# Scatters through disjoint views, routing pieces and gathers moved up, and row numbers kept in order, in an attention and two-layer expert kernel

## The chip, the cores and the metric

One core of a Trainium2 chip runs the whole program. The metric is the device time of one execution in microseconds, from the first to the last instruction plus what lies around them. Engines are named as in the profile: PE is TensorE (matmul) with PEld for its weight loads, DVE is VectorE, ACT is ScalarE, POOL is GpSimd, and SP is SyncE, which here only issues DMAs.

## What is computed

A windowed attention with a few global columns feeds a dense layer with an ELU between two matrices, and its rows feed eight experts, each row going to at most one. In the second part, `x` is the dense layer's output (3072 rows of 512):

```python
do_compute = x @ w_skip > 0
xc = x[do_compute]
logits = xc @ w_gate                      # 8 experts
e_idx = np.argmax(logits, axis=1)
gate_w = softmax(logits)[row, e_idx]
for e in range(8):
    mask = e_idx == e
    h = np.maximum(xc[mask] @ w1[e], 0.0) # 512 -> 1024
    y[mask] = gate_w[mask, None] * (h @ w2[e])
out = x; out[do_compute] = xc + y
```

## The kernel before

The 3072 rows are worked in eight blocks `m` of 384 rows, three tiles of 128 rows each. The main loop (line 872) takes a block in 16 steps `f` of 128 hidden columns: `moe_h` (line 431) is 12 matmuls into `h`, ACT, DVE and POOL turn `h` into the two-part value `gs`, and `moe_y` (line 453) is 9 matmuls that add `gs` times the second matrix into three sums `y`; it runs two steps behind `moe_h` (`LAG`). Attention for the next block is spread over the same steps.

A block's sums are routed by `route` (line 490) in the steps of the next block. Its pieces are: `evac` (ACT copies `y` into a tile `yt` per 128 rows, and the row is written to `out`), `turn` (DVE splits `yt` into two halves, and SP issues a transposing DMA), `gate` (8 small matmuls for the logits of one tile, line 527; behind the third tile's stands `choose`, a run of small DVE instructions that ends in the one-hot tile `oh`, line 548, and the gate weight), `place` (9 small matmuls `rk` count ranks, and DVE makes of them the slot numbers `pos`, line 576), and `scatter` (line 581: POOL issues an indirect DMA that sends the 128 rows of one `yt` to their slots in `xg`, a DRAM tile with 256 rows for each expert). `ROUTE` (line 59) says which piece stands in which step, beginning with step 2. The last block is routed in `ex_tail`, where `ROUTE_LAST` (line 60) names the expert step of each piece.

Experts: `ex_gather` (line 630) loads 128 rows of an expert from `xg` into `yg` by a DMA on SP. `ex_tokens` (line 638) makes a two-part half precision tile `eyh` on DVE (lines 644 and 645; one buffer for all) and has it transposed into `eyT` by a DMA. `ex_first` (line 648) is 12 matmuls into `eh` from `eyT`, after which ACT (line 662) and DVE (line 664) make the two halves of `ehs`; `ex_second` (line 668) is 3 matmuls into `eo`, two steps behind. The third of those three needs the half that DVE makes. At an expert's last step `ex_second` also makes the result row tile on DVE (`eres`, line 684), turns the row numbers into integers (`ix`, line 686, which reads the gathered tile alone) and issues an indirect DMA to `out` on POOL.

`ex_tail` (line 691) first works the first 128 rows of experts 0 to 2 (steps `s_` 0 to 23, eight steps each), and then their second 128 rows (steps 24 to 47). The first 128 rows are known to be filled by the first seven blocks, so they are gathered before the last block is routed: at `f` 11 of the last block, with `ex_tokens` at `f` 13 (line 896). The second 128 rows of those experts are gathered behind the last block's scatters, at step 15, with `ex_tokens` at steps 22, 24 and 26 (lines 709 to 714). Experts 3 to 7 follow with both halves at once. All the while `prep` (line 865) loads and splits one half row of expert weights a step (`ew`, lines 623 and 624); its loads `er` stand in SP's queue too.

What order an engine works in is fixed when the program is compiled. A scheduler takes the instructions in the order of the code, but lets one that its model holds to be ready go ahead of one that is not, and puts in all waits that the tiles' reads and writes need. `pin` (line 72) holds an instruction behind the one written just before it on its engine. On the chip every engine then takes its own list strictly in that order. Two writes to the same DRAM tile are ordered: the later one's issue waits until the earlier one has landed.

Of the kernel before, what the change touches and what calls it, by code (L numbers as in the profile page):

```python
# [1 line left out]

# [10 lines left out]
U32 = DT.uint32  # L13
# [7 lines left out]
B, H, S, D = 4, 8, 768, 64  # L21
NT, DM, FF = 3072, 512, 2048
# [3 lines left out]
TB = 3  # L26
TN = TB * P
NM = NT // TN
# [28 lines left out]
EX_HALVES = (2, 2, 2, 2, 2, 2, 2, 2, 2, 2, 2, 3, 1, 2, 2, 2)  # L57

ROUTE = "ea,b,,cA,B,C,p,x,y,z".split(",")
ROUTE_LAST = {3: 'et', 7: 'A', 8: 'B', 9: 'C', 11: 'p', 12: 'sw'}  # L60


class Fast:
# [400 lines left out]
    def route_init(self):  # L464
        nc = self.nc
        self.wg = self.ct([P, ND, E + 1], F32, "wg")
        nc.sync.dma_start(self.wg[:, :, 0:E], self.a["moe2_w_gate"].rearrange("(c p) e -> p c e", p=P))
        nc.sync.dma_start(self.wg[:, :, E:E + 1], self.a["moe2_w_skip"].rearrange("(c p o) -> p c o", p=P, o=1))

        self.wgs = self.ct([P, ND, 2, E + 1], F16, "wgs")  # L470
        t = self.ct([P, ND, E + 1], F32, "wgt")
        nc.vector.tensor_scalar(t, self.wg, GS, None, ALU.mult)
        nc.vector.tensor_copy(self.wgs[:, :, 0, :], t)
        nc.vector.tensor_tensor(self.wgs[:, :, 1, :], t, self.wgs[:, :, 0, :], ALU.subtract)
        nc.vector.tensor_tensor(t, t, t, ALU.mult)
        self.wgm = self.ct([P, 2], F32, "wgm")
        nc.vector.tensor_reduce(out=self.wgm[:, 0:1], in_=t[:, :, 0:E], op=ALU.max, axis=AX.XY)
        nc.vector.tensor_reduce(out=self.wgm[:, 1:2], in_=t[:, :, E], op=ALU.max, axis=AX.X)
        self.esum = self.ct([P, TB], F32, "esum")
        nc.vector.memset(self.esum, 0.0)  # L480
        self.xg = self.dp.tile([E * CAP, ROW], F32, name="xg")
        z = self.zrow = self.mp.tile([P, ROW], F32, tag="yt", name="zrow", bufs=4)
        nc.gpsimd.memset(z[:, 0:DM + 1], 0.0)
        nc.gpsimd.memset(z[:, DM + 1:ROW], OOB)
# [5 lines left out]
    def route(self, m):  # L490

        nc, mp = self.nc, self.mp
# [87 lines left out]

        def scatter(t):
            nc.gpsimd.indirect_dma_start(
                out=self.xg[:, :], out_offset=bass.IndirectOffsetOnAxis(ap=pos.bitcast(U32)[:, t:t + 1], axis=0),
                in_=yts[t][:, :], in_offset=None, bounds_check=E * CAP - 1, oob_is_err=False)

        def write():
# [4 lines left out]
        if last:  # L591
# [2 lines left out]
                    lambda: [scatter(t) for t in range(TB)], write]  # L594
        ops = dict(e=evac, a=lambda: turn(0), b=lambda: turn(1), c=lambda: turn(2), A=lambda: gate(0), B=lambda: gate(1),
                   C=lambda: gate(2), p=place, x=lambda: scatter(0), y=lambda: scatter(1), z=lambda: scatter(2))
        return [lambda w=w: [ops[o]() for o in w] for w in ROUTE]


    def ex_load(self, e, k):  # L600
# [67 lines left out]
    def ex_second(self, e, f, tiles):  # L668
        nc = self.nc
        hs = self.ehs.pop((e, f, tiles[0]))  # L670
        for j, t in enumerate(tiles):
            if f == 0:
                tag, bufs = ("pv", 1) if (e % 2 and t if e >= NX else e + t == 0) else ("acc", 3)
                self.eo[(e, t)] = self.ps.tile([P, DM], F32, tag=tag, name=f"eo_{e}_{t}", bufs=bufs)
            for n, (s_, x) in enumerate(((0, 0), (0, 1), (1, 0))):
                nc.tensor.matmul(self.eo[(e, t)], hs[:, s_, j * P:(j + 1) * P],  # L676
                                 self.ew[(e, 4 + f // 2, f % 2)][:, x, :],
                                 start=(f == 0 and n == 0), stop=(f == F2 // P - 1 and n == 2))
        if f < F2 // P - 1:
            return  # L680
        for t in tiles:
            y = self.eyg.pop((e, t))
            r = self.mp.tile([P, DM], F32, tag="yT", name=f"eres_{e}_{t}", bufs=2)
            nc.vector.scalar_tensor_tensor(r, self.eo.pop((e, t)), y[:, DM:DM + 1], y[:, 0:DM], ALU.mult, ALU.add)  # L684
            ix = self.xp.tile([P, 1], I32, tag="ix", name=f"ix_{e}_{t}", bufs=2 * E)
            nc.vector.tensor_copy(ix, y[:, DM + 1:DM + 2])
            nc.gpsimd.indirect_dma_start(  # L687
                out=self.out[:, :], out_offset=bass.IndirectOffsetOnAxis(ap=ix.bitcast(U32)[:, 0:1], axis=0),
                in_=r[:, :], in_offset=None, bounds_check=NT - 1, oob_is_err=False)

    def ex_tail(self, prep, rest):
        both = tuple(range(CAP // P))
        steps = [(e, f, (t,)) for t in both for e in range(NX) for f in range(F2 // P)]
        n0 = len(steps)
        steps += [(e, f, both) for e in range(NX, E - 1) for f in range(F2 // P)]
        steps += [(E - 1, f, (t,)) for t in both for f in range(F2 // P)]
        flag = self.flag()
        nf = F2 // P
        pieces = dict(zip("etABCpsw", self.route(NM - 1)))
        for s_, (e, f, tiles) in enumerate(steps):  # L700
            for x in ROUTE_LAST.get(s_, ""):
                pieces[x]()
            if s_ == 0:
                self.htags = "s0", "s1", "h"
            if s_ == 3:
                self.htags = ("h",)
            if s_ == 13:
                self.htags = "h", "s0", "h", "s1"
            if s_ == 15:
                for x in range(NX):  # L710
                    self.ex_gather(x, 1)
            for x in range(NX):
                if s_ == 22 + 2 * x:
                    self.ex_tokens(x, 1)
            if s_ == n0 - 10:
                self.ex_gather(NX, 0)
            if s_ == n0 - 9:
                self.ex_gather(NX, 1)
            if s_ in (n0 - 5, n0 - 3):
                self.ex_tokens(NX, (s_ - n0 + 5) // 2)  # L720
            if len(tiles) == 2 and e + 1 < E:
                if f == 1:
                    for t in both:
                        self.ex_gather(e + 1, t)
                if f in (3, 5):
                    self.ex_tokens(e + 1, (f - 3) // 2)
            self.ex_first(e, f, tiles)
            if s_ and rest:

                self.moe_y(*rest.pop(0))  # L730
            for _ in tiles:
                prep()
            if s_ >= 40:
                next(flag, None)
            if s_ == len(steps) - 1:
                for _ in flag:
                    pass
                self.flag_sum()
            if s_ >= XLAG:
                self.ex_second(*steps[s_ - XLAG])  # L740
        for x in steps[-XLAG:]:
            self.ex_second(*x)
        self.flag_all()
# [80 lines left out]
    def program(self, ep, wp, ap):  # L824
# [26 lines left out]
        t = 0  # L851
# [20 lines left out]
        for s_, (m, f) in enumerate(steps):  # L872
            if m < NM - 1:
                for _ in range(A_STEPS[min(m, 1)].count(f)):
                    self.att_step(t)
                    t += 1
            if m == NM - 1 and f == 0:
                ap.release()
                self.xp = tc.alloc_tile_pool(name="xp", bufs=2)
                self.esums = self.xp.tile([P, 32 * E], F32, tag="esums", name="esums", bufs=1)  # L880
                self.emax = self.xp.tile([P, 2 * E], F32, tag="emax", name="emax", bufs=1)
                nc.gpsimd.memset(self.esums, 0.0)
                for k in range(2):
                    self.ex_load(0, k)
            while done[0] < 2 * f + 2 and m == 0:
                whalf()
            self.moe_h(m, f)
            if m == NM - 1:
                for _ in range(EX_HALVES[f]):
                    prep()  # L890
            if m == 0:
                for _ in range(2):
                    whalf()
            if pend:
                pend.pop(0)()
            if m == NM - 1 and f in (11, 13):
                assert not pend
                for e in range(NX):
                    (self.ex_gather if f == 11 else self.ex_tokens)(e, 0)
            if s_ >= LAG:  # L900
                self.moe_y(*steps[s_ - LAG])
            if m == 0 and f == 7:
                self.route_init()
            if NF // 2 <= s_ < NF // 2 + E * CAP // P:
                self.clear(s_ - NF // 2)
            c = s_ - 2 * NF
            if c == 0:
                self.w_load(0, "wc")
            if 0 < c <= 4 * NF and c % 2 == 0:
                self.w_check(*divmod(c // 2 - 1, 2))  # L910
            if f == LAG and m:
                pend = self.route(m - 1)
                pend.pop(0)()
# [274 lines left out]
```

## Time and profile before

| | us |
|---|---|
| three timed runs | 864.92, 870.45, 873.59 |
| their median | 870.45 |
| the profiled execution | 866.19 |
| its span, first to last instruction | 864.5 |

| engine | busy us | share of the span |
|---|---|---|
| PE | 817.8 | 95% |
| PEld | 479.4 | 55% |
| DVE | 571.4 | 66% |
| ACT | 530.0 | 61% |
| POOL | 174.5 | 20% |

The profile is of one execution. It lists for each instruction when it ran, how long its engine sat idle ahead of it and what ended that. [...] A wait for several things is put down to the one that came last.

### The profile page before, as it was taken

How to read it: one execution, taken by the hardware profiler on the slowest of the kernel's cores; microseconds unless marked ns; L12 is line 12 of the kernel's file. 1: busy time of each engine (PE TensorE's matmuls, PEld its weight loads, DVE VectorE, ACT ScalarE, POOL GpSimd, SP SyncE). 2: the span in 40 equal slices, each digit the busy share in tenths (PEclk: the TensorE clock that was granted, in tenths of full speed). 3: DMA queues.
4: the chain of work that ended last, by engine and by line, in shares of the span. 5: the costliest groups of instructions: out<-in, count | busy, mean ns of one | idle time of the engine just before them, and what ended most of it. 6: DMA issues, size and time to landing. Idle time of an engine off the chain costs nothing.

```text
span 864.5 us, 17637 instructions
## 1 busy us (share of the span) xinstructions
PE 817.8 (95%) x6233; PEld 479.4 (55%) x6233; DVE 571.4 (66%) x1951; ACT 530.0 (61%) x1310; POOL 174.5 (20%) x201
## 2 busy tenths in 40 slices
PE   6997989999999999999999999999998869999995
PEld 4773445555555555555555555555555637666663
DVE  6997997575467567556666765644666846878622
ACT  4775767777767677767776776645655425555311
POOL 1001112123222322321322232232231010101110
PEclk9997999999999999999999999999999988999998
DMA  7999973644686487688659656321646779779510
GB/s 293 256 298 253 245 217 91 132 111 102 201 205 162 137 214 142 175 191 189 152 139 229 154 124 146 77 51 43 189 154 159 228 225 211 247 242 275 157 44 26
DMA packets 185394, 148.80 MB, mean 172 GB/s; under 512 B 152208, under 2 KB 154256, under 8 KB 181200
## 3 DMA queue, kind: packets, MB, share of 16 engines
q1 hardware_dynamic: 182096, 141.59, 63.0%
q0 software_dynamic: 3200, 5.99, 1.9%
q8 instruction: 51, 0.84, 0.4%
q14 instruction: 47, 0.39, 0.2%
HBM read 94.82 MB, written 21.08 MB: 134 GB/s over the span
## 4 chain that ended last, share of the span: by engine, by line
PE 72%; DVE 11%; DMA 10%; issue 4%; POOL 1%; ACT 1%; SPq 0%; POOLq 0%; DVEq 0%; ACTq 0%
PE h L439 25%; PE y L460 24%; PE eh L660 7%; PE eo L676 6%; PE s L239 5%; PE pv L324 4%; DMA eyT<-eyh 3%; DMA xg<-yt,pos 2%; DMA yg<-xg 2%; DVE ew L624 2%; DVE wt L408 2%; DVE wt L409 1%; PE warm L354 1%; DMA xT<-xs 1%; DVE w L416 1%
## 5 line engine op out<-in xcount | busy, mean ns | idle before, releaser
L439 PE MATMUL h<-xT,w 128*128 128x384 f16 x1536 | 274.9, 329 | 4.1 <-DMA xT<-xs 4.1
L460 PE MATMUL y<-w,gs 128*128 128x512 f16 x1152 | 271.4, 381 | 0.0
L439 PEld LDWEIGHTS <-w 128*128 128x128 f16 x1536 | 146.8, 99 | 106.4 <-issue 9.7
L450 POOL TENSOR_TENSOR gs<-e,gs 128x384 f16<-128x384 f32 x128 | 126.1, 987 | 393.9 <-ACT gs L449 329.2
L460 PEld LDWEIGHTS <-gs 128*128 128x128 f16 x1152 | 110.8, 98 | 119.9 <-issue 2.7
L446 DVE SCALAR_TENSOR_TENSOR e<-e,h 128x384 f32<-128x384 f32 x128 | 70.4, 551 | 99.6 <-ACT e L444 94.1
L449 ACT ACTIVATE gs<-e 128x384 f16<-128x384 f32 x128 | 66.7, 522 | 86.1 <-DVE e L446 84.9
L253 ACT ACTIVATE p<-p,st 128x232 f32<-128x232 f32 (+1 forms) x192 | 89.2, 465 | 38.4 <-DVE st L248 37.7
L660 PE MATMUL eh<-eyT,ew 128*128 128x128 f16 (+1 forms) x1152 | 103.6, 243 | 7.6 <-DMA eyT<-eyh 5.6
L676 PE MATMUL eo<-ew,ehs 128*128 128x512 f16 x384 | 102.0, 388 | 8.1 <-DVE ehs L664 8.1
L660 PEld LDWEIGHTS <-ew 128*128 128x128 f16 x1152 | 88.7, 101 | 32.8 <-issue 6.7
L624 DVE SCALAR_TENSOR_TENSOR ew<-er,ew 128x512 f16<-128x512 f32 x128 | 90.5, 725 | 15.9 <-ACT ew L623 14.5
L443 ACT ACTIVATE e<-h 128x384 f32<-128x384 f32 x128 | 61.6, 481 | 58.5 <-PE h L439 54.5
L662 ACT ACTIVATE ehs<-eh 128x128 f16<-128x128 f32 (+1 forms) x96 | 29.9, 311 | 102.3 <-PE eh L660 99.8
L248 DVE CUSTOM_DVE_ANT_0 p<-s,tab 128x232 f32<-128x232 f32 (+1 forms) x192 | 67.1, 377 | 20.3 <-PE s L239 18.6
L623 ACT ACTIVATE ew<-er 128x512 f16<-128x512 f32 x128 | 75.4, 620 | 4.5 <-DMA er<-in_moe_w 4.2
L283 DVE TENSOR_TENSOR ph<-p,ph 128x464 f16<-128x464 f32 x68 | 43.1, 648 | 40.2 <-ACT ph L282 40.2
L444 ACT ACTIVATE e<-e 128x384 f32<-128x384 f32 x128 | 66.6, 520 | 2.5
L664 DVE SCALAR_TENSOR_TENSOR ehs<-eh,ehs 128x128 f16<-128x128 f32 (+1 forms) x96 | 31.9, 332 | 36.9 <-ACT ehs L662 36.7
L676 PEld LDWEIGHTS <-ehs 128*128 128x128 f16 x384 | 35.4, 99 | 36.7 <-DVE ehs L664 12.7
L687 POOL DMA_INDIRECT out<-eres,ix x16 | 16.9, 1053 | 161.9 <-DVE eres L684 117.7
L239 PE MATMUL s<-qh 64*128 64x232 f16 (+1 forms) x432 | 40.0, 254 | 3.1 <-DVE st L248 2.5
(171 smaller groups left out, 849.4 us busy)
## 6 DMA issues: line engine op xcount, KB each, us to landing
er<-in_moe_w SPq DMA_DIRECT2D x64, 512.0 KB
wr<-in_wf SPq DMA_DIRECT2D x16, 1024.0 KB
wc<-in_wf SPq DMA_DIRECT2D x16, 1024.0 KB
qk<-in_qk SPq DMA_DIRECT2D x20, 720.0 KB
out<-yt SPq DMA_DIRECT2D x24, 256.0 KB
rawv<-in_vp SPq DMA_DIRECT2D x21, 256.0 KB
xg<-zrow SPq DMA_DIRECT2D x16, 257.0 KB
yg<-xg SPq DMA_DIRECT2D x16, 257.0 KB
```

The costliest lines, as they stand in the source:

```text
L239: nc.tensor.matmul(sp[j], q[r, hp, KW:], k[r, hp, KW - w:KW], start=(x == 0), stop=(x == len(mm) - 1))
L248: nc.vector.tensor_tensor_reduce(pw[:, j, :], sp[j], self.tab[:, h, :] if i else self.tab0[:, h, :], -0.125, 3e38, ALU.add, ALU.min, st[:, ...
L253: nc.scalar.activation(pw[:, j, :], pw[:, j, :], AF.Exp, bias=st[:, 0, h:h + 1], scale=-1.0, accum_out=st[:, 1, h:h + 1])
L439: nc.tensor.matmul(hps, wi[:, s_, c, :], xT[:, x * ND + c, :], start=(n == 0), stop=(n == 3 * ND - 1))
L446: nc.vector.scalar_tensor_tensor(g, e, -HS, hps, ALU.mult, ALU.max, accum_out=self.gsum[:, m * NF + f:m * NF + f + 1])
L449: nc.scalar.activation(gs[:, 0], g, AF.Copy)
L450: nc.gpsimd.tensor_tensor(gs[:, 1], g, gs[:, 0], ALU.subtract)
L460: nc.tensor.matmul(self.ys[m][t], gs[:, s_, t * P:(t + 1) * P], wo[:, x, :], start=(f == 0 and n == 0), stop=(f == NF - 1 and n == 2))
L623: self.pin(nc.scalar.activation(w[:, 0], r, AF.Copy, scale=sc))
L624: nc.vector.scalar_tensor_tensor(w[:, 1], r, sc, w[:, 0], ALU.mult, ALU.subtract, accum_out=self.esums[:, c:c + 1])
L660: nc.tensor.matmul(hps, l, r, start=(i == 0), stop=(i == len(mm) - 1))
L676: nc.tensor.matmul(self.eo[(e, t)], hs[:, s_, j * P:(j + 1) * P], self.ew[(e, 4 + f // 2, f % 2)][:, x, :], start=(f == 0 and n == 0), sto ...
```

## The change

There are three edits.

1. The scatters write through `xgs`, three views of `xg` that are declared disjoint, one for each tile of a block. Scatters of different tiles are no longer ordered against each other; a gather still reads `xg` itself and waits for all three.
2. Pieces are moved. For the last but one block (`m` 6) the routing follows `ROUTE_NEXT`: the third `turn` stands one step earlier, the gates and `place` stay at `f` 5 to 8, and all three scatters stand at `f` 9 in place of 9, 10 and 11. The first gathers go from `f` 11 to 10 and their `ex_tokens` from 13 to 12. In `ROUTE_LAST` the gates go from steps 7, 8, 9 to 6, 7, 8, `place` from 11 to 9, the scatters from 12 to 10, and the write of the rows stays at 12. The second gathers go from step 15 to 13, and their `ex_tokens` from 22, 24 and 26 to 17, 20 and 23.
3. The row number conversion `ix` is pinned behind `eres`, the instruction written before it on DVE.

```diff
--- before.py
+++ after.py
@@ -2,6 +2,7 @@
 
 import concourse.bass as bass
 import concourse.tile as tile
+from concourse.bass_types import dram_disjoint_views
 from concourse import mybir
 from concourse._compat import with_exitstack
 from concourse.masks import make_identity
@@ -57,7 +58,8 @@
 EX_HALVES = (2, 2, 2, 2, 2, 2, 2, 2, 2, 2, 2, 3, 1, 2, 2, 2)
 
 ROUTE = "ea,b,,cA,B,C,p,x,y,z".split(",")
-ROUTE_LAST = {3: 'et', 7: 'A', 8: 'B', 9: 'C', 11: 'p', 12: 'sw'}
+ROUTE_NEXT = "ea,b,c,A,B,C,p,xyz".split(",")
+ROUTE_LAST = {3: 'et', 6: 'A', 7: 'B', 8: 'C', 9: 'p', 10: 's', 12: 'w'}
 
 
 class Fast:
@@ -479,6 +481,8 @@
         self.esum = self.ct([P, TB], F32, "esum")
         nc.vector.memset(self.esum, 0.0)
         self.xg = self.dp.tile([E * CAP, ROW], F32, name="xg")
+
+        self.xgs = dram_disjoint_views(self.xg[:, :], TB)
         z = self.zrow = self.mp.tile([P, ROW], F32, tag="yt", name="zrow", bufs=4)
         nc.gpsimd.memset(z[:, 0:DM + 1], 0.0)
         nc.gpsimd.memset(z[:, DM + 1:ROW], OOB)
@@ -580,7 +584,7 @@
 
         def scatter(t):
             nc.gpsimd.indirect_dma_start(
-                out=self.xg[:, :], out_offset=bass.IndirectOffsetOnAxis(ap=pos.bitcast(U32)[:, t:t + 1], axis=0),
+                out=self.xgs[t][:, :], out_offset=bass.IndirectOffsetOnAxis(ap=pos.bitcast(U32)[:, t:t + 1], axis=0),
                 in_=yts[t][:, :], in_offset=None, bounds_check=E * CAP - 1, oob_is_err=False)
 
         def write():
@@ -594,7 +598,7 @@
                     lambda: [scatter(t) for t in range(TB)], write]
         ops = dict(e=evac, a=lambda: turn(0), b=lambda: turn(1), c=lambda: turn(2), A=lambda: gate(0), B=lambda: gate(1),
                    C=lambda: gate(2), p=place, x=lambda: scatter(0), y=lambda: scatter(1), z=lambda: scatter(2))
-        return [lambda w=w: [ops[o]() for o in w] for w in ROUTE]
+        return [lambda w=w: [ops[o]() for o in w] for w in (ROUTE if m < NM - 2 else ROUTE_NEXT)]
 
 
     def ex_load(self, e, k):
@@ -683,7 +687,7 @@
             r = self.mp.tile([P, DM], F32, tag="yT", name=f"eres_{e}_{t}", bufs=2)
             nc.vector.scalar_tensor_tensor(r, self.eo.pop((e, t)), y[:, DM:DM + 1], y[:, 0:DM], ALU.mult, ALU.add)
             ix = self.xp.tile([P, 1], I32, tag="ix", name=f"ix_{e}_{t}", bufs=2 * E)
-            nc.vector.tensor_copy(ix, y[:, DM + 1:DM + 2])
+            self.pin(nc.vector.tensor_copy(ix, y[:, DM + 1:DM + 2]))
             nc.gpsimd.indirect_dma_start(
                 out=self.out[:, :], out_offset=bass.IndirectOffsetOnAxis(ap=ix.bitcast(U32)[:, 0:1], axis=0),
                 in_=r[:, :], in_offset=None, bounds_check=NT - 1, oob_is_err=False)
@@ -706,11 +710,11 @@
                 self.htags = ("h",)
             if s_ == 13:
                 self.htags = "h", "s0", "h", "s1"
-            if s_ == 15:
+            if s_ == 13:
                 for x in range(NX):
                     self.ex_gather(x, 1)
             for x in range(NX):
-                if s_ == 22 + 2 * x:
+                if s_ == 17 + 3 * x:
                     self.ex_tokens(x, 1)
             if s_ == n0 - 10:
                 self.ex_gather(NX, 0)
@@ -893,10 +897,10 @@
                     whalf()
             if pend:
                 pend.pop(0)()
-            if m == NM - 1 and f in (11, 13):
+            if m == NM - 1 and f in (10, 12):
                 assert not pend
                 for e in range(NX):
-                    (self.ex_gather if f == 11 else self.ex_tokens)(e, 0)
+                    (self.ex_gather if f == 10 else self.ex_tokens)(e, 0)
             if s_ >= LAG:
                 self.moe_y(*steps[s_ - LAG])
             if m == 0 and f == 7:
```

## Rows read from the trace of the kernel before

**Rows 1.** windows of 24 us: window, busy us (instructions) per engine, TensorE clock, DMA share, GB/s

```profile
192.00:216.00 24.00, 23.96 (x181) 12.91 (x180) 13.67 (x47) 18.05 (x45) 7.95 (x8) 1.00 0.47 107
...
648.00:672.00 24.00, 20.55 (x138) 12.00 (x136) 16.86 (x56) 13.81 (x30) 3.65 (x4) 0.93 0.63 165
...
696.00:720.00 24.00, 15.15 (x126) 9.76 (x125) 11.37 (x45) 7.32 (x19) 3.90 (x4) 0.72 0.84 202
```

**Rows 2.** the same windows, cut to 5 us

```profile
660.00:665.00 5.00, 4.89 (x33) 3.52 (x34) 3.71 (x10) 2.93 (x7) 0.91 (x1) 0.66 0.58 107
...
715.00:720.00 5.00, 5.00 (x47) 3.97 (x46) 3.06 (x14) 3.07 (x8) 0.00 (x0) 0.68 1.24 162
```

**Rows 3.** timeline of PE: start, us, what [idle before it, and who ended that]

```profile
422.54 2.11 PE L460 MATMUL y<-w,gs 128*128 128x512 f16 x9
...
660.11 2.68 PE L660 MATMUL eh<-eyT,ew 128*128 128x128 f16 x24 [2.56 <-DMA eyT<-eyh]
...
673.11 0.83 PE L660 MATMUL eh<-eyT,ew 128*128 128x128 f16 x12 [2.00 <-DVE ehs L664]
...
680.44 0.25 PE L530 MATMUL lg<-wgs,yTa 128*128 128x18 f16 x4
...
686.77 0.83 PE L660 MATMUL eh<-eyT,ew 128*128 128x128 f16 x12
...
700.61 0.59 PE L676 MATMUL eo<-ew,ehs 128*128 128x512 f16 x2
...
706.09 1.46 PE L676 MATMUL eo<-ew,ehs 128*128 128x512 f16 x3 [4.88 <-DVE ehs L664]
...
713.55 4.00 PE L660 MATMUL eh<-eyT,ew 128*128 128x128 f16 x36 [3.09 <-DMA eyT<-eyh]
```

**Rows 4.** chain of work that ended last, from 600 us: start, us, what

```profile
606.12 1.95 PE h L439 x12
608.07 1.94 PE y L460 x9
...
655.54 4.52 DMA eyT<-eyh
...
689.11 6.46 DMA xg<-yt,pos
...
696.32 3.00 DMA xg<-yt,pos
...
700.07 2.83 DMA xg<-yt,pos
...
703.92 4.07 DMA yg<-xg
```

**Rows 5.** timeline of DVE, columns as for PE

```profile
645.69 0.15 DVE L686 CAST ix<-yg 128x1 int32<-128x1 f32 x1 [3.85 <-DMA yg<-xg]
...
654.37 0.42 DVE L644 TENSOR_SCALAR eyh<-yg 128x512 f16<-128x512 f32 x1
...
661.23 0.55 DVE L446 SCALAR_TENSOR_TENSOR e<-e,h 128x384 f32<-128x384 f32 x1
...
688.19 0.16 DVE L576 TENSOR_TENSOR pos<-sm 128x3 int32<-128x3 f32 x1
...
705.67 0.15 DVE L686 CAST ix<-yg 128x1 int32<-128x1 f32 x1 [6.78 <-DMA yg<-xg]
```

**Rows 6.** timeline of POOL: a middle block, then the last scatter's successor

```profile
419.48 1.50 POOL L450 TENSOR_TENSOR gs<-e,gs 128x384 f16<-128x384 f32 x1 [0.25 <-ACT gs L449]
...
701.34 0.97 POOL L687 DMA_INDIRECT out<-eres,ix  x1 [0.30 <-issue]
```

**Rows 7.** the instructions on tile xg: time from issue to landing of the 24 scatters

```profile
DMA to landing us min/median/max: 2.4/3.4/7.9
```

**Rows 8.** timeline of SP, the transposing issues of the last block

```profile
671.04 3.98 SPq L522 DMA_TRANSPOSE yTa<-yha  x3
```

**Rows 9.** timeline of ACT, a weight half that waited for its load

```profile
695.75 0.63 ACT L623 ACTIVATE ew<-er 128x512 f16<-128x512 f32 x1 [1.25 <-DMA er<-in_moe_w]
```

## The prediction

> **What bounds the kernel now.** I read the windows of the whole span first, to see where PE, the busiest engine, isn't full. From 144 to 648 us it is: one of the 21 windows there, all alike, shows 23.96 of 24 us [rows 1]. So nothing that the change does in those blocks can gain; it can only lose. From 648 on PE loses: 20.55 of 24, and 15.15 in the window that starts at 696 [rows 1]. [...] PE's timeline then gives the places [rows 3], the chain says what PE waited for [rows 4], and the timelines of DVE, POOL, SP and ACT say what held that up [rows 5 to 9].
>
> The losses of PE, one after the other:
> - *Loss a, at 660.11*, step 0 of the expert steps: 2.56 of wait for the first `eyT` [rows 3], then 0.34 of the window at 660 in clock, 1.7 [rows 2]. Sum 4.3.
> - *Loss b, at 673.11*, step 5: 2.00 of wait for `ehs` of DVE. A step, 12 matmuls and 3, takes (700.61 − 686.77 − 0.65)/10 = 1.32: ten steps lie between step 13 at 686.77 and step 23, and 0.65, a third of 1.95 [rows 4], is step 23's own 12 matmuls ahead of 700.61. From 673.11 to 680.44, the third gate at step 9, four steps and two gates would take 5.5 and took 7.3 [rows 3]: 1.8 more. Sum 3.8.
> - *Loss c, from 700.61 to 713.55*, the change from the first to the second 128 rows: 12.9, of which nine `ex_second` matmuls, as many and as wide as those of a `moe_y` (1.94 [rows 4]), are work; 11.0 lost. DVE stood 6.78 on one `ix` that waited for a gather, with the `ehs` that PE wanted behind it (PE's wait of 4.88); then PE waited for `eyT` [rows 3, 5]. The clock then costs 0.32 of 5 us, 1.6 [rows 2]. Sum 12.6.
>
> Behind loss c stands one line: `pos` done at 688.35 [rows 5], three scatters in turn, 689.11, 696.32 and 700.07 with 6.46, 3.00 and 2.83 to land [rows 4], the gathers at 702.9, the first of them in at 705.67 [rows 5], and the transposing.
>
> **Part by part.** Everything is costed in the profiled execution.
>
> *First gathers and tokens earlier, ix pinned (loss a).* `ex_tokens` ran at 654.37 by its place in DVE's list; the gather was in by 645.69, where an `ix`, let ahead, held DVE for 3.85 [rows 5]. One `f` earlier is 1.95 + 1.94 = 3.9 [rows 4], so 650.5; the transposing follows 1.17 later and takes 4.52 [rows 4]: `eyT` at 656.2, PE asks at 660.11 − 2.56 = 657.55. The wait goes, with 1.35 to spare, more if DVE also wins the 3.85. The scatters in front of it have room: two are gone from the series, so this gather isn't later than 645.69. Late next is the last `e` at 661.23 [rows 5], which stands among the three `ex_tokens`; these share one buffer, so each waits for the transposing before it. PE now comes 4.2 sooner for its result. Nothing lost if `e` keeps its place, up to 3.4 if the third `ex_tokens` comes in front of it (5.8 of transposing and split, less 2.4 of room, my estimate from the same rows); I take 1.0, nearer nothing. Gain 4.3 − 1.0 = 3.3.
>
> *Loss b.* DVE was late because the third `ex_tokens`, weight halves and the three `turn` pieces came together. The `ex_tokens` goes earlier, the rest stays. Between 0 and 3.8 I take half, 1.9.
>
> *Gates and place.* SP issues the three `yTa` transposings from 671.04 over 3.98 [rows 8]; the first gate stood two steps with their gates ahead of the third, 680.44 − 3.0 = 677.4, 6.4 behind. One step (1.32) and half of the slow clock (0.9) less leaves 4.2 against a landing of 4.52: a wait of 0.3, none to 1.6; 0.5 taken. The third gate then comes at 680.44 − 3.3 − 1.9 − 1.3 + 0.5 = 674.4. `place` needs `oh`, and DVE is full here: from 680.44 to 686.77 PE took 0.7 more than its steps, the wait for `oh`. `place` now stands one step nearer to the gate: 0.7 more to 2.0 if PE's list keeps the code's order, 0.7 if the scheduler puts it later, as it put three `ex_first` behind the `ex_second` after them (x36 at 713.55) [rows 3]; an extra 0.5 taken. `pos` came 7.9 behind the third gate, and DVE's instructions are the same: 682.3.
>
> *Scatters in flight together (loss c).* The first is issued 0.8 later (689.11 − 688.35) [rows 4, 5], 683.1. POOL's pitch is 701.34 − 700.07 = 1.27 [rows 4, 6], so the third goes at 685.6. It lands 2.83 to 6.46 later [rows 4]; over all 24 it was 2.4 to 7.9 [rows 7]. I take 4.5, between, because three move at once: 690.1, where it was 702.9.
>
> [...]
>
> *Second gathers and tokens.* A gather is in 2.8 after its issue (705.67 − 702.9) [rows 5]: 692.9. From there to the transposing it took 713.55 − 4.52 − 705.67 = 3.4, with two more `ix` in front; bounds 1.2 to 3.4, 1.9 taken: 694.8, and `eyT` at 699.3. PE without waits: 674.4 + (700.61 − 680.44) + 1.3 + 0.5 = 696.4, plus 1.95 of `ex_second`: 698.3. Wait 1.0. For the clock behind it 0.4 (none to 1.6). So the second rows start in effect at 699.7 where it was 713.55 + 1.6: 15.4 gained in all, a, b and c together.
>
> *SP's queue.* The gathers stand in front of later weight loads and hold SP until 690.1. A half already waited 1.25 for its load [rows 9], and ACT takes `ehs` behind it. If SP comes to the gathers at step 14 (682.5) it is held 7.6; loads stand four steps, 5.3, ahead. None to 5; 1.2 taken, since a part falls under the wait for `eyT`.
>
> *ix at the end.* After the last `eres` one 0.15 copy is added [rows 5]: 0.1 lost. Elsewhere it costs nothing: DVE has idle time under PE. *The moved third turn* of block 6 is hidden too: PE is full there.
>
> Sum: 15.4 − 1.2 − 0.1 = 14.1. The profiled execution took 866.19 with 1.69 outside the span, untouched: 852.1. The median of the runs, 870.45, is 4.3 above it; 14.1 less gives 856.
>
> **Rivals.** *The three scatters gain nothing together.* If the last still lands 13.8 after the first issue, at 696.9, `eyT` comes at 706.1; 6.8 and 1.2 of clock are lost again, less the 1.2 of SP, now hidden: gain 7.3, 863. For it: the 6.46 with loads beside it [rows 4]. Against it: 3.00 and 2.83.
>
> *A new stall takes ix's place.* The pinned `ex_tokens` stands in DVE's list where the scheduler's model has the gather landed; `ix` shows it to be 6.78 too early [rows 5]. DVE would stand on `ex_tokens`, and SP on the gathers with weights behind. Much of this falls into the time in which PE waits for `eyT` anyway; SP's 5 in full gives a gain of 9: 861.
>
> *POOL is held by the scatters, slower.* In seven blocks the three issues may now stand together in front of POOL's `gs`. In a middle block that ends at 419.48 + 1.50 = 420.98 [rows 6], and `y` starts at 422.54, with 0.43 until its third matmul, the first to need it [rows 3]: room 2.0. Two more issues are 2.54: 0.5 a block, 3.8 in all, still a gain. If POOL takes the next issue only when the former has landed, two medians of 3.4 [rows 7] make 6.8 − 2.0 = 4.8 a block and 34 in all: 890. It decides from 14.1/7 = 2.0 a block. Against it: POOL issued at 701.34 while the scatter of 700.07 was still in flight (it landed at 702.9) [rows 4, 6].
>
> [...] No row here shows an issue stretched to a landing.
>
> **How the numbers follow.** The forecast has 0.68: gain 10 to 18 by the terms' bounds, most of which lie on one path and don't add; 852 to 861, 856 likeliest. No gain from scatters together: 0.13. New stall: 0.12. POOL: 0.07. A measurement here tells about 1%, 8.7 us, from no change: faster needs 861.7 or less, which is the forecast and under half of the new stall, 0.72. Within 1%: 0.21. Slower: 0.07. The three runs spread 4 to either side, so the range is 848 to 866: it takes in the first two rivals and leaves out POOL's and part of the edges.
>
> **What would show it.** Right: no idle PE of 2 us at step 0; three scatters within 3 us of each other and all landed within 8; no DVE wait on `ix`; idle before the second rows of 1 to 4 us in place of 11, at a clock near 1. Wrong: an `ex_tokens` or a weight half with a wait of 5 us or more ahead of it; the third scatter landing 10 us behind the first issue; waits of PE in `moe_y` behind scatters.

## The result, and the profile after

The changed kernel takes 871.26 us in the median of 20 runs, the kernel before 865.89 in as many beside them: a ratio of 1.0059, with a 95% interval of 1.0035 to 1.0083. It is a little slower, by less than 1%, where 856 and a ratio of 0.983 were foretold. The kernel before itself ran 4.6 us under the 870.45 of the three runs shown ahead.

The profiled execution of the changed kernel took 866.84, with a span of 865.1, and lies 4.4 under its own median, so the losses it shows may be smaller than those of a usual run. PE's timeline (start, us, what, idle before it and who ended that) shows every stall of 0.9 us and more behind 660 us, and one of 0.65 among them:

```profile
665.35 0.60 PE L462 MATMUL y<-w,gs 128*128 128x512 f16 x2 [0.90 <-ACT gs L451]
673.39 0.83 PE L664 MATMUL eh<-eyT,ew 128*128 128x128 f16 x12 [2.08 <-DVE ehs L668]
681.45 0.38 PE L569 MATMUL rk<-oh,tri 128*128 128x8 f16 x9 [0.93 <-DVE oh L552]
697.64 0.39 PE L680 MATMUL eo<-ew,ehs 128*128 128x512 f16 x1 [2.61 <-DVE ehs L668]
699.79 0.39 PE L680 MATMUL eo<-ew,ehs 128*128 128x512 f16 x1 [0.65 <-DVE ehs L668]
702.24 1.39 PE L680 MATMUL eo<-ew,ehs 128*128 128x512 f16 x3 [1.40 <-ACT ehs L666]
785.17 2.74 PE L664 MATMUL eh<-eyT,ew 128*128 128x256 f16 x12 [4.82 <-DMA eyT<-eyh]
810.23 1.47 PE L664 MATMUL eh<-eyT,ew 128*128 128x256 f16 x12 [2.76 <-DMA eyT<-eyh]
```

The first six answer to [rows 3]: the waits for the first and for the second `eyT` are gone, and between the first and the second rows PE is idle for 4.7 us (2.61, 0.65 and 1.40), where [rows 3] alone have 4.88 and 3.09. The last two are new. They stand at the first step of expert 5 and of expert 6, where the timeline of the kernel before lists no idle PE. The windows (us, then busy us and instructions of PE, PEld, DVE, ACT, POOL, then the clock granted to TensorE as a share of the full one, DMA share and GB/s) say the same: 20.12 for the 15.15 of [rows 1], and 19.18 one stage later, with the clock lower right behind the first new wait:

```profile
696.00:720.00 24.00, 20.12 (x199) 13.08 (x200) 17.88 (x73) 11.36 (x29) 2.35 (x2) 0.93 1.04 289
768.00:792.00 24.00, 19.18 (x123) 12.45 (x122) 13.66 (x49) 10.10 (x21) 0.97 (x1) 0.93 0.75 228
785.00:790.00 5.00, 4.83 (x27) 3.27 (x28) 1.55 (x7) 1.42 (x3) 0.00 (x0) 0.72 0.71 279
```

Four marks on PE's timeline split the span: `rk` of block 0 and of block 6, the start of step 0 less the wait ahead of it, the first step of expert 3 (the first `eh` of 256 columns), and `flagp` at the end.

| stretch, us | before | after | difference |
|---|---|---|---|
| to `rk` of block 0 | 190.43 | 192.05 | +1.6 |
| `rk` of block 0 to `rk` of block 6 | 437.54 | 438.87 | +1.3 |
| to step 0 | 29.58 | 29.42 | −0.2 |
| step 0 to expert 3 | 91.45 | 79.46 | −12.0 |
| expert 3 to `flagp` | 106.32 | 115.51 | +9.2 |

So 12.0 us were gained where the prediction looked for 14, and 9.2 lost where it looked for nothing. Of the 9.2, the two waits are 7.6. The 1.6 lie ahead of all that the change moves; in the 14 profiles of the experiments this mark lay between 189.56 and 192.33 with no relation to the edits. The gains and losses of these two profiles cancel: both reach `flagp` at the same time, 855.32 and 855.31. The 5.4 us between the two medians are not seen in them, and where they lie stays open: no other execution of the changed kernel has a trace.

**Where the new waits come from.** DVE's timeline of the changed kernel around the end of expert 3, and SP's with the issues of DMAs (line, kind, what):

```profile
764.23 0.75 DVE L688 SCALAR_TENSOR_TENSOR eres<-eo,yg 128x512 f32<-128x512 f32 x1
766.11 0.15 DVE L690 CAST ix<-yg 128x1 int32<-128x1 f32 x1
766.18 0.74 DVE L688 SCALAR_TENSOR_TENSOR eres<-eo,yg 128x512 f32<-128x512 f32 x1
766.84 0.14 DVE L690 CAST ix<-yg 128x1 int32<-128x1 f32 x1
...
771.61 0.43 DVE L648 TENSOR_SCALAR eyh<-yg 128x512 f16<-128x512 f32 x1 [1.29 <-DMA yg<-xg]
...
778.82 0.43 DVE L648 TENSOR_SCALAR eyh<-yg 128x512 f16<-128x512 f32 x1 [2.90 <-issue]
```

```profile
766.65 0.94 SPq L639 DMA_DIRECT2D yg<-xg  x2
...
773.32 1.23 SPq L650 DMA_TRANSPOSE eyT<-eyh  x1
...
780.48 1.23 SPq L650 DMA_TRANSPOSE eyT<-eyh  x1
```

The same place in the kernel before, DVE and then SP:

```profile
773.42 0.75 DVE L684 SCALAR_TENSOR_TENSOR eres<-eo,yg 128x512 f32<-128x512 f32 x1
775.31 0.75 DVE L684 SCALAR_TENSOR_TENSOR eres<-eo,yg 128x512 f32<-128x512 f32 x1
777.53 0.43 DVE L644 TENSOR_SCALAR eyh<-yg 128x512 f16<-128x512 f32 x1
...
783.00 0.43 DVE L644 TENSOR_SCALAR eyh<-yg 128x512 f16<-128x512 f32 x1
```

```profile
774.20 0.33 SPq L635 DMA_DIRECT2D yg<-xg  x1
...
776.08 0.33 SPq L635 DMA_DIRECT2D yg<-xg  x1
```

The gathered rows of expert 5 go into `yt` buffers that expert 3's rows leave. Before, `ix` had long been read when `eres` was made, so `eres` was the last reader: the gather follows its start by 0.78. After, the pinned `ix` reads `yg` too, and for the first tile it stands behind two weight halves, 1.9 behind `eres`: the gather follows `eres` by 2.42, both gathers go out together, and what comes behind is later at each step. Counted from the first `eres`, the weighings start at 7.4 and 14.6 where it was 4.1 and 9.6. Before, there was little to spare: if the second transposing took the 4.64 there that it took after (an estimate), `eyT` was in at 784.19 + 4.64 = 788.8, and PE came to it at 789.38. The experiments try whether this is the cause.

### The profile page after: what moved, and what is told of

Read it like the earlier page. It is cut to its first block, busy times and chain, and to the rows that moved or that the text cites. A ratio compares the mean times of both kernels' runs of the same rounds, so it can differ in the third digit from the quotient of the medians.

```text
span 865.1 us, 17637 instructions
## 1 busy us (share of the span) xinstructions
PE 815.2 (94%) x6233; PEld 476.6 (55%) x6233; DVE 569.1 (66%) x1951; ACT 530.1 (61%) x1310; POOL 171.9 (20%) x201
## 4 chain that ended last, share of the span: by engine, by line
PE 75%; DVE 10%; DMA 7%; issue 4%; POOL 2%; ACT 1%; SPq 0%; POOLq 0%; DVEq 0%; ACTq 0%
PE h L441 25%; PE y L462 24%; PE eh L664 7%; PE eo L680 7%; PE s L241 5%; PE pv L326 4%; DMA eyT<-eyh 3%; PE warm L356 2%; DVE wt L411 1%; DVE wt L410 1%; DMA xT<-xs 1%; DVE ew L628 1%; DVE e L448 1%; DVE w L418 1%; POOL xg L586 1%
## 5 line engine op out<-in xcount | busy, mean ns | idle before, releaser
L452 POOL TENSOR_TENSOR gs<-e,gs 128x384 f16<-128x384 f32 x128 | 123.2, 965 | 432.1 <-ACT gs L451 365.0
L664 PEld LDWEIGHTS <-ew 128*128 128x128 f16 x1152 | 86.6, 99 | 35.5 <-issue 6.2
```

The costliest lines, as they stand in the source:

```text
L452: nc.gpsimd.tensor_tensor(gs[:, 1], g, gs[:, 0], ALU.subtract)
L664: nc.tensor.matmul(hps, l, r, start=(i == 0), stop=(i == len(mm) - 1))
```

## The experiments

Theory A: the pinned copy, as last reader of `yg`, frees `yt` late, and this makes the new waits. Theory B: the gathers, scatters and weighings that were moved up make them, and the pin costs nothing. Each run's ratio is to the kernel before on the same chip.

| run | ratio, 95% interval | step 0 to expert 3 | expert 3 to `flagp` |
|---|---|---|---|
| before | 1 | 91.45 | 106.32 |
| changed kernel | 1.0059 (1.0035 to 1.0083) | 79.46 | 115.51 |
| e1 change without pin | 0.996 (0.9942 to 0.9977) | 83.58 | 106.32 |
| e2 pin alone | 1.0082 (1.0059 to 1.0105) | 85.40 | 119.51 |
| e3 change, copy early | 0.9933 (0.9916 to 0.995) | 83.63 | 106.32 |
| e4 change, copy ahead of `eres` | 1.0082 (1.0058 to 1.0105) | 80.37 | 117.65 |
| e5 moved pieces alone | 0.9955 (0.9934 to 0.9976) | 83.81 | 106.32 |
| e6 views alone | 0.9996 (0.9974 to 1.0019) | 87.57 | 106.33 |
| e7 before, copy early | 0.9989 (0.9968 to 1.001) | 85.66 | 106.32 |
| e8 e3, weighings spread | 0.9949 (0.9928 to 0.9969) | 82.22 | 106.32 |
| e9 change, copy from a tile of its own | 0.9951 (0.9929 to 0.9973) | 85.77 | 107.32 |
| e10 copy late for 3 experts, then early | 0.9922 (0.99 to 0.9943) | 83.02 | 106.32 |
| e11 e3, views for two blocks | 0.9907 (0.9874 to 0.9941) | 81.90 | 106.32 |
| e12 e10, views for two blocks | 0.9914 (0.9885 to 0.9944) | 80.42 | 106.33 |
| e13 e11, two more buffers for `eyh` | 0.993 (0.991 to 0.9951) | 79.02 | 106.32 |
| e14 e5, copy early | 0.9932 (0.9911 to 0.9952) | 82.28 | 106.32 |

**The pin: e1 to e4, e9.**

```diff
 e1_nopin
-            self.pin(nc.vector.tensor_copy(ix, y[:, DM + 1:DM + 2]))
+            nc.vector.tensor_copy(ix, y[:, DM + 1:DM + 2])
```

> The changed kernel without the pin: the copy that makes the row numbers (ix) may go where the scheduler puts it. Theory A (the pinned copy is now the last reader of the gathered rows yg, so it frees the yt buffers later, the gathers of the experts after the next start 2 us later and close together, and TensorE waits 4.82 us for eyT at the start of expert 5 and 2.76 us at expert 6): both waits are gone, and the time is 7 to 9 us under the changed kernel's, about 863 where that stands at 871, so about 0.996 of the kernel before. Theory B (the lateness comes from the gathers and scatters that were moved up, and the pin costs nothing): the waits at experts 5 and 6 stay, and the time is the changed kernel's, 1.006 of the kernel before.

Without the pin the waits at experts 5 and 6 are gone, the last stretch is before's 106.32, and the ratio falls from 1.0059 to 0.996, 8.6 us of 866. Theory A said 7 to 9, B none. From step 0 to expert 3 its profile is 4.1 longer than that of the changed kernel, so the two profiles lie only 5.4 apart at `flagp`.

e2 is the kernel before with the same line pinned, and nothing else.

> The kernel before with the pin alone: scatters on the whole buffer and nothing moved. Theory A: the gathers of experts 5 and 6 are late here too; before, their rows were there about 1 us ahead of need, so TensorE waits 3.5 to 5 us at expert 5 and up to 3 at expert 6, and the kernel is 5 to 9 us slower than the kernel before (1.006 to 1.010). Against that stands the 6.78 us that DVE waits for ix near the end, off the path as foretold (0.1 us). Theory B: no wait at experts 5 and 6, the same time as the kernel before (0.999 to 1.001).

PE's timeline has both waits, a little longer than foretold, without any of the moved pieces:

```profile
787.87 2.74 PE L660 MATMUL eh<-eyT,ew 128*128 128x256 f16 x12 [5.06 <-DMA eyT<-eyh]
815.01 1.60 PE L660 MATMUL eh<-eyT,ew 128*128 128x256 f16 x12 [3.96 <-DMA eyT<-eyh]
```

7 us slower than before, and theory B falls. But the pin does good ahead of that: from step 0 to expert 3 this kernel is 6.0 shorter than before, and its wait for the first `eyT` is 0.36. No `ix` stands on a gather in front of the weighings any more; DVE weighs the first tile at 651.59, which before it did at 654.37 [rows 5].

```diff
 e3_ixearly
         nc.vector.scalar_tensor_tensor(yh[:, 1], y, RS, yh[:, 0], ALU.mult, ALU.subtract)
+        ix = self.xp.tile([P, 1], I32, tag="ix", name=f"ix_{e}_{t}", bufs=2 * E)
+        self.pin(nc.vector.tensor_copy(ix, self.eyg[(e, t)][:, DM + 1:DM + 2]))
+        self.eix[(e, t)] = ix
...
-            ix = self.xp.tile([P, 1], I32, tag="ix", name=f"ix_{e}_{t}", bufs=2 * E)
-            self.pin(nc.vector.tensor_copy(ix, y[:, DM + 1:DM + 2]))
+            ix = self.eix.pop((e, t))
```

> The changed kernel with the row numbers copied, pinned, right behind the weighing of a tile's gathered rows (eyh), so ahead of the experts' products, not behind the residual sum (eres). It keeps ix in order, but eres is again the last reader of yg. Theory A: no wait at experts 5 and 6, time 7 to 9 us under the changed kernel's (about 0.995 of the kernel before). Theory B: the waits stay and the time is that of the changed kernel.

In order and early: 0.9933, no wait at experts 5 and 6.

e4 writes the pinned copy ahead of `eres` instead of behind it.

> The changed kernel with the pinned copy written ahead of the residual sum instead of behind it; in DVE's order both copies then stand behind the two halves of ew and ahead of eres. Theory A, if it is the last read of yg alone that counts: eres follows the copy by one instruction, so the buffers come free at about the changed kernel's time, and the waits at experts 5 and 6 stay within 1 us of the 4.82 and 2.76 us there: time within 2 us of the changed kernel's. If instead the pin's place among DVE's other work (the weighing eyh and the halves of ew and ehs that move around it) makes the lateness, the waits change by more than that with the new order. Theory B: no change from the changed kernel.

The waits stay, 5.50 and 3.27, and the time can't be told from the changed kernel's. But DVE's order is not the one foretold: the first `eres` still starts at 765.28, ahead of the two weight halves, and both copies at 767.17, behind them. So the copy is still the last reader of the first tile, and e4 doesn't tell its place from its read.

So far the late place of the copy and its reading `yg` go together. e9 parts them:

```diff
 e9_ixcopy
+        nc.scalar.activation(fx, self.eyg[(e, t)][:, DM + 1:DM + 2], AF.Copy, scale=1.0)
+        self.efx[(e, t)] = fx
...
-            self.pin(nc.vector.tensor_copy(ix, y[:, DM + 1:DM + 2]))
+            self.pin(nc.vector.tensor_copy(ix, self.efx.pop((e, t))))
```

> The changed kernel with the pinned copy left where it is, behind eres, but reading a small tile of its own, into which ScalarE copies the column of row numbers when the tile is weighed. So DVE still makes ix late and in order, and only the reader of yg is gone. If the release of yt by the last reader makes the waits at experts 5 and 6: both gone, time near that of the early pinned copy, 0.992 to 0.996 of the kernel before. If the place of the pinned copy in DVE's list makes them: waits of 4.82 and 2.76 us as in the changed kernel, 1.006.

DVE's timeline, and SP's:

```profile
770.75 0.75 DVE L691 SCALAR_TENSOR_TENSOR eres<-eo,yg 128x512 f32<-128x512 f32 x1
772.63 0.15 DVE L693 CAST ix<-fx 128x1 int32<-128x1 f32 x1
772.70 0.74 DVE L691 SCALAR_TENSOR_TENSOR eres<-eo,yg 128x512 f32<-128x512 f32 x1
```

```profile
771.52 0.33 SPq L639 DMA_DIRECT2D yg<-xg  x1
...
773.47 0.33 SPq L639 DMA_DIRECT2D yg<-xg  x1
```

The copy is as late as in the changed kernel, 1.9 behind `eres`, and the gather is out before it, 0.77 behind `eres`. The wait at expert 5 is gone, the ratio 0.9951. At expert 6, where none was expected, 0.84 of 2.76 are left, and why stays open. For the rest it is the last read of `yg` that costs, not the copy's place.

**What the moved pieces and the views are worth: e5 to e7, e14.** e5 is the kernel before with `ROUTE_NEXT`, `ROUTE_LAST` and the four changed step numbers; e6 with the views alone; e7 with e3's edit alone; e14 with e5's and e3's.

> The kernel before with the moved routing pieces, gathers and weighings alone: no pin, scatters on the whole buffer, one behind the other. If the scatters in flight together are worth what stands between before's 13.8 us and the changed kernel's 8.6 us from the first issue to the last landing, this kernel lies 4 to 5 us above the changed kernel without the pin (which ran at 0.996 of the kernel before), so at 1.000 to 1.002 of the kernel before; its waits for the first eyT at 660 should be gone if the moved gathers removed them. If the scatters' overlap was hidden anyway, it runs as the changed kernel without the pin, 0.996.

> The kernel before with the scatters through disjoint views alone. The scatters of blocks 0 to 6 then follow one another on POOL at 1.3 to 1.8 us and hold the multiplication gs behind them: that costs 0.9 us over three blocks in the changed kernel's trace. The last block's scatters land 5 us earlier and, with nothing else moved, the second gathers start as much earlier, which should take 4 to 5 us off the wait before the second rows. Together 3 to 4 us faster, 0.995 to 0.997 of the kernel before. If the gathers were not limited by the scatters, 1.000 to 1.002.

> The kernel before with the row numbers copied, pinned, right behind the weighing of a tile, ahead of the products; nothing else changed. In the kernel with the pin alone expert 3 began 6.7 us earlier than in the kernel before (742.27 against 749.00), since no ix copy stood ahead of the weighings in DVE's order, and that was lost again at experts 5 and 6, where the pinned copy freed yt late. With the copy early both hold: about 5 to 7 us faster than before, 0.992 to 0.994. If the early start of expert 3 came from elsewhere, 0.999 to 1.001.

> The kernel before with the moved pieces and the early pinned copy, but no views at all: the last block's scatters run one behind the other too. If the scatters in flight together give their foretold 4 to 5 us once the pin is mended, this kernel lies that much above the one with views for the last two blocks (0.991): 0.995 to 0.997. If the earlier gathers only lead to an earlier wait of the second rows, it is level with it: 0.990 to 0.993.

The moved pieces alone give all that the change without its pin gives, 0.9955 and 0.996; views on top of them bring nothing that these runs can tell, and neither do they alone (0.9996, where 0.995 to 0.997 were expected). e7 missed too, with 0.9989. In the single profiles of e6 and e7 the stretch from step 0 to expert 3 is 3.9 and 5.8 shorter than before, but 12 runs of each show no such gain. e14 lies between its two forecasts: its 0.9932 is 2 us above e11's 0.9907, with intervals that overlap, so it may be level with e11 or have lost a part of the 4 to 5 us.

The views do what they say. POOL's timeline of e14, one scatter behind the other, and then the chain of waits of the changed kernel with its last scatter, issued 2.68 behind the first at 685.57, and what follows:

```profile
681.78 0.97 POOL L583 DMA_INDIRECT xg<-yt,pos  x1 [0.65 <-ACT ehs L666]
687.17 0.97 POOL L583 DMA_INDIRECT xg<-yt,pos  x1 [4.42 <-ACT ehs L666]
694.10 0.97 POOL L583 DMA_INDIRECT xg<-yt,pos  x1 [5.96 <-ACT ehs L666]
```

```profile
688.25 5.89 DMA xg<-yt,pos
694.14 0.02 issue
694.16 2.77 DMA yg<-xg
...
698.22 5.36 DMA eyT<-eyh
```

But the lead is given back. e11 and e14 differ by the views of the last two blocks alone. DVE starts the first of the second rows' weighings, L648 and L645, at 694.34 in e11 and at 699.58 in e14, after waits of 3.44 and 7.25 for the gather; from step 0 to expert 3 e11 is 0.4 shorter.

The views also cost. Three scatters then stand together in front of POOL's `gs`, and in blocks 2 to 4 `gs` is late for PE. PE's timeline has `rk` of block 2 and of block 5 in the kernel before, in the changed one, and in e11, which has views for the last two blocks alone:

```profile
339.31 0.37 PE L565 MATMUL rk<-oh,tri 128*128 128x8 f16 x9
563.46 0.37 PE L565 MATMUL rk<-oh,tri 128*128 128x8 f16 x9
```

```profile
340.93 0.37 PE L569 MATMUL rk<-oh,tri 128*128 128x8 f16 x9
...
349.72 1.68 PE L462 MATMUL y<-w,gs 128*128 128x512 f16 x7 [0.19 <-POOL gs L452]
...
566.41 0.37 PE L569 MATMUL rk<-oh,tri 128*128 128x8 f16 x9
```

```profile
339.16 0.37 PE L569 MATMUL rk<-oh,tri 128*128 128x8 f16 x9
563.27 0.37 PE L569 MATMUL rk<-oh,tri 128*128 128x8 f16 x9
```

224.15, 225.48 and 224.11: 1.33 us for three blocks, gone in e11. Three issues in a row alone don't cost it: from `rk` of block 0 to `rk` of block 2 it is 148.88 in both kernels. POOL's timeline of the changed kernel in block 1 and in block 2, and DVE's:

```profile
272.26 0.97 POOL L586 DMA_INDIRECT xg<-yt,pos  x1 [0.30 <-issue]
...
345.93 1.52 POOL L586 DMA_INDIRECT xg<-yt,pos  x1 [0.31 <-issue]
```

```profile
272.31 0.90 DVE L207 TENSOR_TENSOR qh<-qk,qh 128x720 f16<-128x720 f32 x1
...
345.69 0.90 DVE L207 TENSOR_TENSOR qh<-qk,qh 128x720 f16<-128x720 f32 x1
```

In block 1 the second issue starts just ahead of DVE's `qh` and takes 0.97. In block 2 it starts while `qh` runs, takes 1.52 and ends 0.86 behind `qh`; blocks 3 and 4 are alike (0.84 and 0.85). With these 0.55 `gs` comes too late for PE; in block 1, without them, it doesn't. That `qh` holds the issue up is argued from the times and was not tried.

```diff
 e11_ixearly_late
-                out=self.xgs[t][:, :], out_offset=...
+                out=(self.xgs[t] if m >= NM - 2 else self.xg)[:, :], out_offset=...
```

> The changed kernel with the early pinned copy, and disjoint views for the last two blocks alone; blocks 0 to 5 scatter into the whole buffer, one scatter behind the other, as before. From the routing of block 0 to that of block 6 the four kernels with whole-buffer scatters took 437.5 to 438.4 us and the six with views 438.8 to 439.1, in three steps of 0.44 us. If that is POOL's burst of three scatters in front of gs, this kernel takes 1.3 us less than the early copy (0.9933 of before), so 0.990 to 0.993, and its stretch is 437.5. If not, the stretch stays at 438.9.

e11 runs at 0.9907, faster than both kernels by the interval; from e3's 0.9933 it can't be told in time, though its trace is 1.2 shorter there.

**Where the rest goes: e8, e10, e12, e13.** Without the late release 3.5 to 8 us are gained where 14 were foretold. In e1 a new wait stands behind the gathers, in DVE's timeline and 2 us later in PE's:

```profile
713.32 0.43 DVE L648 TENSOR_SCALAR eyh<-yg 128x512 f16<-128x512 f32 x1 [4.32 <-DMA eyT<-eyh]
```

```profile
715.38 0.61 PE L680 MATMUL eo<-ew,ehs 128*128 128x512 f16 x1 [3.31 <-DVE ehs L668]
```

The weighing of the third tile waits until the transposing of the second has read the one `yh`, and `ehs` queues behind it on DVE. e8 moves the weighings apart (`17 + 6 * x` for `17 + 3 * x`), e10 keeps the copy late for the first three experts as in the change, e12 adds the views for two blocks alone, e13 gives `eyh` the two buffers that `xT` leaves.

> The changed kernel with the early pinned copy (ran at 0.993 of before) and the weighings of the second rows at steps 17, 23 and 29 instead of 17, 20 and 23. There DVE stood 5.28 us at 707.88 in a weighing whose buffer yh the last transposing still read, and TensorE then waited 4.38 us at 715.27 for ehs. With the weighing later DVE goes on with ehs meanwhile: 3 to 5 us faster than the early pinned copy alone, 0.988 to 0.990 of before. If the stall goes to another place (the gathers of expert 3, or eyT of the third tile), 0.993.

> The changed kernel with the pinned copy behind eres for the first three experts, as in the change, and early, right behind the weighing, for the others. The changed kernel takes 79.46 us from the first step of expert 0 to the first of expert 3, the one with the early copy 83.63 (a wait of 4.38 us at 715.27). If that difference is the order of DVE's work in this stretch, this kernel has the short stretch and no waits behind it: 4 us under the early copy, 0.988 to 0.990 of before. If it is chance of the transfers, 0.992 to 0.995.

> Both together: late pinned copy for the first three experts, early for the others, and views for the last two blocks alone. If both gains hold, 5 us under the early copy with views throughout: 0.986 to 0.989 of before. If neither, 0.992 to 0.995.

> The kernel with the early pinned copy and views for the last two blocks alone (0.991 of before), with the weighed rows eyh of the second tiles and of the later experts in the two buffers xT, free by then, instead of the one buffer yh. If the rest of the foretold gain is lost because each weighing waits on DVE until the transposing before it has read yh (5 to 9 us each, in whose shadow ehs is late and TensorE waits 1.55 us at 711.53 in that kernel and 3.3 to 5.1 us in its sisters), these waits go and the stretch from expert 0 to expert 3 shrinks from 81.9 us to 78 to 80: 0.986 to 0.989. If the transfers are the limit themselves, the wait moves to eyT and the time stays at 0.990 to 0.992.

e8 has no wait at 715, but 2.24 at 730.98 and 0.72 at 741.09; 0.9949, no gain over e3. e10 still has the wait, 4.50 at 713.11, so that order of copies alone doesn't give the short stretch of the changed kernel; e12 has 3.32 at 710.03. e10 and e12, which have the same edits in this stretch, differ by 2.6 there, so a difference of 2 to 3 us between two single profiles says little. In e13 the weighings of the second and third tile start 3.5 apart without a wait, and the next one waits for its own gather:

```profile
709.27 0.43 DVE L651 TENSOR_SCALAR eyh<-yg 128x512 f16<-128x512 f32 x1 [3.09 <-DMA yg<-xg]
```

PE's wait moves with it, 2.50 at 709.96. Its stretch of 79.02 is 2.9 under e11's, as foretold, but the ratio is 0.993, and its interval overlaps that of e11: no gain in time is shown. Each cure moves the wait on to the next transfer. What these waits have in common, gathers, transposings and weight loads under way together at a high DMA share (1.04 in the changed kernel's window at 696), is argued and not tried; whether it sets the length of this stretch stays open.

## Why the prediction was wrong, point by point

**The step that failed is the one on `ix`**: "Elsewhere it costs nothing: DVE has idle time under PE." It priced the copy by its 0.15 us on DVE and not by what it reads. The copy holds `yg` until it has run, `yg` holds a `yt`, and a `yt` is what the gather of the expert after next waits for. By e1 the pin costs 8.6 us in time; in the trace the stretch from expert 3 on is 9.2 longer. The same step missed a gain: by e2 the pin alone takes loss a away but for 0.36, which the prediction had put down to the earlier first gathers; either does (e5 has no wait there).

**Loss a.** Right: the wait for the first `eyT` is gone, the clock behind it is 1.00. In its place come 0.90 for `gs` at 665.35 and 0.39 a microsecond later, 1.3 in all, where 1.0 was taken, and for the reason given: the last `e` (664.18) stands behind the third weighing, which began at 663.11 after a wait of 1.37.

**Loss b.** The wait itself was not shortened, 2.08 for 2.00 [rows 3]; the slow steps behind it went, the clock being 1.00 from 672 to 700. The prediction's 1.8 for them is rather 1.6: with 0.21 for each of the two gates (677.40 to 677.61 on PE's timeline before), four steps and two gates take 5.7, not 5.5. So the size, 1.9, nearly came out by luck: the wait that was to shrink stayed, and why the clock held is not shown.

**Gates and place.** No wait at the gates (0.5 taken), 0.93 ahead of `rk` (0.5 extra taken). Of the 0.7 that the prediction read as the wait of the kernel before, its timeline lists 0.46 as idle; most of the rest is `rk` itself.

**Scatters together.** The right kind of gain: 2.68 from the first issue to the last, 8.57 from the first issue to the last landing, for 13.8 before. 7.0 was foretold, since a scatter among three was taken to land in 4.5 and the last took 5.89. Over all 24 scatters the median from issue to landing rose from 3.4 [rows 7] to 5.3, and it is 3.3 to 4.1 in the five profiles without views and 5.3 to 7.7 in the eight with views for all blocks: in flight together each took longer, and the last block's three still ended 5.2 sooner. On the whole kernel no gain is shown: e5 without views is level with e1, and e14 and e11 can't be told apart.

**Second gathers.** `eyT` of the second rows was foretold at 699.3 and came at 703.58. Of these 4.3, 2.8 were there before the stretch began: the forecast counts from 657.55, and step 0 came at 660.34. Counted from there the first scatter was issued 0.3 sooner than foretold and the last landed 1.2 later; the gather took 2.77 (2.8 taken), the transposing 5.36 (4.52). DVE stood 4.60 on the gather with `ehs` behind, the mechanism of the second rival in a mild form, and PE waited 2.61 and 0.65.

*SP's queue.* Right in kind: the weight loads stood behind the gathers, which SP issued at 694.16. ACT then stood 7.80 on a weight half, with `ehs` behind it, and PE waited 1.40; 1.2 was taken. The waits of the two engines, DVE's and ACT's:

```profile
696.95 0.43 DVE L648 TENSOR_SCALAR eyh<-yg 128x512 f16<-128x512 f32 x1 [4.60 <-DMA yg<-xg]
```

```profile
701.39 0.63 ACT L627 ACTIVATE ew<-er 128x512 f16<-128x512 f32 x1 [7.80 <-DMA er<-in_moe_w]
```

The second is one of the signs that the prediction had named for being wrong. Together PE lost 4.7 where 1.0 and 1.2 were foretold, and the clock behind it was 0.75 from 700 to 705. From step 0 to expert 3 this leaves a gain of 12.0, where the sum had 14.2.

**POOL.** The bound of 0.5 a block stood under the third rival and was left out of the sum; 0.44 in each of three blocks were measured. No scatter held POOL until it landed, and the longest issue took 1.52, so the third rival's worse half fell. In blocks 2 to 4, where `qh` was already running, an issue took 1.52 in place of the 0.97 of block 1; no run shows why.

**The rivals and the range.** None of the rivals was what happened as a whole. The range ended at 866 because the two that it took in kept some gain, and the one that lost, POOL's, was left out. The second rival's gain of 9 doesn't come out of its terms: SP's 5 in full for the 1.2 leaves 10.3. A rival of the form "a buffer is freed by a later reader" needed only the question that the prediction asked of every other moved step and not of this one: what is late next.

## What to carry to other kernels

A pinned instruction is priced by what it reads: if it becomes the last reader of a rotating buffer, it moves the transfer that waits for that buffer, however short it is itself (0.15 us here, 8.6 in time by e1). Copy a small field out where the data arrives, and the buffer is freed by the work that needs the rest of it (e3, 0.9933). And a transfer made early in a stage whose next transfers queue for one buffer, here at a DMA share of 1.01 to 1.12 from 695 to 710 in e11, can give most of its lead back: counted from step 0 (657.19 and 658.68), e11's first weighing of the second rows starts 3.75 ahead of e14's, and 0.4 of it are left at expert 3. Look for the next wait in each of those transfers before the lead is counted.

## What was not expected of the hardware

After 4.82 us of idle PE at 785.17 the clock is granted at 0.72 over 5 us; after 2.76 at 810.23 it isn't lowered (1.00 from 810 to 815). The length of the idle stretch alone doesn't decide it: behind the 2.00 before [rows 3] the clock was 0.61 from 673 to 677, behind the 2.08 after it was 1.00.

And a high DMA share need not mean that much is moved: in e9 the window from 708 to 712 has a share of 1.45 and 92 GB/s, in the changed kernel the same 4 us have 1.17 and 295. In both a transposing was issued 2 us earlier; the weighing that waits for its buffer started 8.9 us behind that issue in e9, and 5.0 in the changed kernel. What makes the difference is not known.

```profile
708.00:712.00 4.00, 3.73 (x41) 2.36 (x38) 0.48 (x4) 1.31 (x3) 0.00 (x0) 1.00 1.45 92
```

```profile
708.00:712.00 4.00, 4.00 (x48) 2.94 (x46) 2.08 (x8) 2.39 (x6) 0.00 (x0) 1.00 1.17 295
```
